# The two copies that empty a group's turned logits are handed out ahead of the next unit's two mask copies

## The chip, the cores and the metric

One core of a Trainium2 chip runs the whole program. The metric is the device time of one execution in microseconds (us); lower is better. Before the change the median of three runs is 447.19 us.

## What is computed

Three layers follow one another on 3072 tokens (4 batches of 768) of width 384 (8 heads of 48):

```python
# 1: a linear recurrence over time, per batch and head, state D x D
y[t]  = r[t] @ (state + (u * k[t]) outer v[t])
state = w * state + k[t] outer v[t]
# 2: soft mixture, 8 experts of 4 slots = 32 slots
logits     = x @ phi                                   # 3072 x 32
slot_input = softmax(logits, over tokens).T @ x        # 32 x 384
slot_out   = relu(slot_input @ w1[e]) @ w2[e]
x          = softmax(logits, over slots) @ slot_out
# 3: an MLP
h = x @ w_in;  out = (h * sigmoid(1.702 * h)) @ w_out  # 384 -> 2048 -> 384
```

All is float32.

## The kernel before

**Layer 1 and the logits of layer 2** run in one loop over 24 units. A unit is 128 tokens of one batch, with all 8 heads; units of two batches alternate. The recurrence is computed in chunks: inside a unit by masked products (TensorE makes `pa`, a mask cuts it to the triangle, the result is `am`), across units by a state (`u_ps`, `sc`, `sbd`). The loop is software-pipelined: step `n` (L652, from -2 to 25) handles several units at different stages, as `st_a(n + 1)`, `st_v(n)`, `st_n(n - 1)`, `k_turn(n + 2)`. The order in which the code stands is the order on each engine's queue: nothing reorders it (a manual schedule), and an engine that waits at one instruction holds back all behind it.

The steps that matter here, in the order of one pass of the loop:

- `r_decay(n + 2)` (L493): VectorE scales `rt` of a later unit.
- `st_a(n + 1)` (L505 to L523): TensorE makes the masked products `pa` in two banks (L512); VectorE copies one bank into `am` under the mask (L516, a predicated copy), ScalarE copies the other bank (L519), and GpSimd cuts that one to the triangle (L520). `am` of unit `n + 1` is read by `st_v(n + 1)` (L612), one step of the loop later.
- `st_q(n + 1)` (L529, L532): TensorE sums for the bonus term into `k_ps`, ScalarE copies them to `qT`.
- `bonus`, `st_n` (L547, L551), `k_turn` (L499, L502, L503), `st_y`, `st_u`, `st_v`, `st_s`, `st_x`.

Every four units make a **group** `g` of the mixture's logits. Its work is spread over two steps of the loop. In the first one (`n = 4g + 5`) TensorE makes the logits, `maxima` takes their running maximum and the exponentials `et`, and `rows(g, (0,))` turns `et` and the plain logits `ls` on TensorE into one bank, `ltp` (L204, L205). In the second (`n = 4g + 6`) `rows(g, (1,))` empties this bank by two copies: VectorE takes the exponentials to `en` (L209), ScalarE the logits to `lnat` (L210). Then `sums(g, ..., n=(0,))` makes the weighted sums `pp` on TensorE from `en` (L221). `lp`, `ltp`, `pp` are one after the other in the same bank (tag `l`, one buffer), so `pp` waits for both copies. In the instruction order before, ScalarE's copy `lnat` carries a wait for VectorE, whose copy `en` reads the same bank; and `bonus(n)` on GpSimd writes the `xn` slot that `pp` reads, so it waits for `pp`. Groups 0 to 4 go this way, at n = 6, 10, 14, 18 and 22; group 5 is handled behind the loop by `slot_inputs`.

In the same loop VectorE and ScalarE decode `w_in` (L87 to L107, three steps a pass) and SyncE hands out the loads of the weights.

**After the loop** come a branch on a flag (L711, its body is skipped with these inputs), the experts, whose weights and `w_out` are loaded meanwhile, and the **MLP**, which is two thirds of the time and a nearly unbroken row of matmuls (L1124).

Of the kernel before, what the change touches and what calls it, by code (L numbers as in the profile page):

```python
# [21 lines left out]
def attn_moe_mlp_kernel(  # L22
# [275 lines left out]
    with ExitStack() as actx:  # L298
# [60 lines left out]
        with tc.manual_schedule():  # L359
# [119 lines left out]
            def ok(i):  # L479
                return 0 <= i < NU  # L480
# [3 lines left out]
            def k_decay(i, eng=nc.gpsimd):  # L484
                if ok(i):
                    eng.tensor_tensor(
                        out=kp[i % NKP][:, :, 0:D], in0=kv[i % NKV][:, 0], in1=tab, op=ALU.mult
                    )

            def r_decay(i):  # L490
                if ok(i):
                    x = rt[i % NRT]
                    tt(out=x, in0=x, in1=tr, op=ALU.mult)  # L493

            def k_turn(i):

                if ok(i):
                    for q in range(NP):
                        nc.tensor.transpose(  # L499
                            k_ps[:, q, :], kp[i % NKP][:, 2 * q:2 * q + 2, :].rearrange("p h d -> p (h d)"), ident  # L500
                        )
                    nc.scalar.copy(out=kT, in_=k_ps)  # L502
                    tt(out=rk, in0=rt[i % NRT], in1=k_ps, op=ALU.mult)  # L503

            def st_a(i):  # L505

                if ok(i):
                    t = [ps.tile([P, NP, P], F32, tag="a", name="pa", bufs=2) for _ in range(2)]
                    for q in range(NP):
                        for m in range(2):  # L510
                            p = slice(HP * m, HP * m + D)
                            nc.tensor.matmul(  # L512
                                t[m][:, q, :], kT[p, q, :], rt[i % NRT][p, q, :], start=True, stop=True
                            )
                    x = am[i % NA]
                    nc.vector.copy_predicated(  # L516
                        out=x[:, 0], mask=mask.unsqueeze(1).to_broadcast([P, NP, P]), data=t[0]
                    )
                    nc.scalar.copy(out=x[:, 1], in_=t[1])  # L519
                    nc.gpsimd.affine_select(  # L520
                        out=x[:, 1], in_=x[:, 1], pattern=[[0, NP], [1, P]], compare_op=ALU.is_gt, fill=0.0,
                        base=0, channel_multiplier=-1,
                    )  # L523

            def st_q(i):

                if ok(i):
                    for q in range(NP):
                        nc.tensor.matmul(  # L529
                            k_ps[NS * q:NS * q + NS, 0, :], ubd[:, q, :], rk[:, q, :], start=True, stop=True  # L530
                        )
                    nc.scalar.copy(out=qT, in_=k_ps[:, 0, :])  # L532

            def bonus(i):
                if ok(i):
                    nc.gpsimd.tensor_tensor(
                        out=xn[:, i % NXN, 0:DM].rearrange("p (q m d) -> p q m d", m=2, d=D),
                        in0=kv[i % NKV][:, 1].rearrange("p (q m) d -> p q m d", m=2),
                        in1=xq[(i - 1) % NXT][:, DM:].rearrange("p (q m) -> p q m", m=2)
                        .unsqueeze(3).to_broadcast([P, NP, 2, D]), op=ALU.mult,  # L540
                    )

            def st_n(i):

                if ok(i):
                    for q in range(NP):
                        nc.tensor.transpose(  # L547
                            n_ps[:, 2 * q:2 * q + 2, :].rearrange("p h d -> p (h d)"), yT[:, q, :], ident
                        )
                    x = xn[:, i % NXN, 0:DM].rearrange("p (h d) -> p h d", d=D)  # L550
                    tt(out=x, in0=n_ps[:, :, 0:D], in1=x, op=ALU.add)  # L551
# [17 lines left out]
            def st_u(i):  # L569
                if ok(i) and units[i][1] < NC - 1:  # L570
                    for q in range(NP):
                        for m in range(2):
                            h = 2 * q + m
                            nc.tensor.matmul(
                                u_ps[HP * m:HP * m + HP, q, :], kp[i % NKP][:, h, :], kv[i % NKV][:, 1, h, :],
                                start=True, stop=True,
                            )

            def st_s(i):

                if not ok(i) or units[i][1] == NC - 1:
                    return
                b, c = units[i]
                s = sc[b % 2]
                wb = w128.unsqueeze(2).to_broadcast([P, NP, D])
                if c == 0:
                    tt(out=s, in0=u_ps, in1=wb, op=ALU.mult)
                else:
                    tt(out=s, in0=u_ps, in1=s, op=ALU.add)
                    tt(out=s, in0=s, in1=wb, op=ALU.mult)  # L590
                for m in range(2):
                    p = slice(HP * m, HP * m + HP)
                    nc.scalar.copy(out=sbd[b % 2][p, :, m, 0:D], in_=s[p])

            def st_y(i):
                if not ok(i):
                    return
                b, c = units[i]
                if c > 0:
                    for q in range(NP):  # L600
                        nc.tensor.matmul(  # L601
                            y_ps[:, q, :], sbd[b % 2][:, q].rearrange("p m d -> p (m d)"), rt[i % NRT][:, q, :],
                            start=(q == 0), stop=False, skip_group_check=True,
                        )

            def st_v(i):
                if not ok(i):
                    return
                c = units[i][1]
                for q in range(NP):  # L610
                    for m in range(2):
                        nc.tensor.matmul(  # L612
                            y_ps[HP * m:HP * m + D, q, :], kv[i % NKV][:, 1, 2 * q + m, :], am[i % NA][:, m, q, :],
                            start=(c == 0 and q == 0), stop=(q == NP - 1), skip_group_check=True,
                        )
                nc.scalar.copy(out=yT, in_=y_ps)  # L616

            def g1(g):
                grp.products(
                    g,  # L620
                    [[(phn[:, kk, :], xq[(4 * g + m + 1) % NXT][:, kk * P:(kk + 1) * P]) for kk in range(KD)]
                     for m in range(4)],
                )

            def g3_x(g):
                return [xn[:, (4 * g + m) % NXN, :] for m in range(4)]
# [25 lines left out]
            for n in range(-2, NU + 2):  # L652
                g, m = divmod(n - 5, 4)
                first, second = (0 <= g < NG and m == x for x in range(2))
                second = second and g < NG - 1
                r_decay(n + 2)
                st_a(n + 1)
                if second:
                    grp.rows(g, (1,))
                st_q(n + 1)  # L660
                if first:
                    g1(g)
                if second:
                    grp.sums(g, g3_x(g), n=(0,))
                bonus(n)
                st_n(n - 1)
                k_turn(n + 2)
                if first:
                    grp.maxima(g)
                if second:  # L670
                    grp.sums(g, None, n=(1,))
                st_y(n)
                st_u(n)
                st_v(n)
                st_s(n)
                st_x(n)
                if first and g < NG - 1:
                    grp.rows(g, (0,))
                k_decay(n + 3, nc.gpsimd if n > -1 else nc.vector)
                if n == 1:  # L680
                    flag()
                    flag_out()
                    selector()
                if n == 4:
                    n_ok = nc.values_load(flg, min_val=0, max_val=P * NP)
                if n >= 0:
                    ld_r(n + NRT)
                    ld_kv(n + NKV)
                wload(n)
                if n == NU - 1:  # L690
                    while eq:
                        load_w(*eq[0], wts, eq[0][0])
                        eq.pop(0)
                    for a in (2, 3):
                        load_w(NSL, a, wts, NSL)
# [514 lines left out]
```

## Time and profile before

| | |
|---|---|
| runs | 447.01, 447.19, 450.7 us |
| profiled execution | 451.58 us, of which the span of its instructions is 450.1 us |
| mean granted TensorE clock | 0.968 of full speed |
| busy, share of the span | TensorE 93%, VectorE 59%, ScalarE 42%, GpSimd 14% |
| the loop over the units | up to about 172 us of the span |
| branch, experts, loading of `w_out` | about 172 to 224 us |
| MLP | about 224 us to the end |

In the rows further down, times are microseconds from the span's start. A row of the timeline gives the start, the duration, the engine, the line, the operation with its output and inputs, and in square brackets how long the engine had been idle before it and whom it waited for. Starts of consecutive instructions on VectorE and ScalarE may lie a few hundredths of a microsecond before the end of the one ahead. PE is TensorE, PEld its weight loads, DVE VectorE, ACT ScalarE, POOL GpSimd, SPq the queue of SyncE that issues DMAs.

### The profile page before, as it was taken

Reading aid. Unit: us, or ns where it says so; the run is one execution under the profiler, and the core shown is the slowest. Engines: PE = TensorE matmul, PEld = TensorE weight load, DVE = VectorE, ACT = ScalarE, POOL = GpSimd, SP = SyncE. Lnnn points to the kernel's source line nnn. Section 1 sums busy time; section 2 is a strip of 40 time slices with the busy share of each in tenths; the row PEclk is TensorE's granted clock in tenths of the full one; section 3 lists DMA queues with packets and bytes.
Section 4 is the critical chain, followed back from the end, with each engine's and each line's share of the span. In section 5 each row is a group of like instructions: output and inputs, shape, how many; then the busy total and the mean of one; then the engine's idle time right before and its main releaser. Section 6 shows DMA issues by size and latency. Waiting matters only on the chain.

```text
span 450.1 us, 9164 instructions
## 1 busy us (share of the span) xinstructions
PE 417.3 (93%) x3704; PEld 363.0 (81%) x3704; DVE 265.3 (59%) x497; ACT 189.3 (42%) x444; POOL 61.0 (14%) x89
## 2 busy tenths in 40 slices
PE   7899899898989976996799999999999999999996
PEld 5687687676767853442499999999999999999996
DVE  6467788777879754304669995444454444544442
ACT  3345655455555631423458776222242222322321
POOL 4244334342433220000000000000000000000000
PEclk9589999999999998898999999999999999999999
DMA  7345788777867364799233200200011000110003
GB/s 253 114 146 178 254 267 274 235 257 259 270 223 233 109 229 163 252 381 379 93 109 108 69 1 6 100 0 1 0 46 61 1 0 1 66 40 0 1 0 106
DMA packets 36000, 59.50 MB, mean 132 GB/s; under 512 B 3056, under 2 KB 21616, under 8 KB 35952
## 3 DMA queue, kind: packets, MB, share of 16 engines
q1 hardware_dynamic: 35952, 58.85, 39.2%
q8 instruction: 32, 0.52, 0.5%
q14 instruction: 16, 0.13, 0.1%
HBM read 53.53 MB, written 4.72 MB: 129 GB/s over the span
## 4 chain that ended last, share of the span: by engine, by line
PE 54%; DMA 2%; DVE 2%; ACT 1%; SPq 1%; issue 1%; DVEq 0%; ACTq 0%
PE o L1124 45%; PE hpa L1062 3%; DMA raw_a<-in_moe_w_out_dram 2%; PE hp L819 2%; PE hpb L1062 2%; PE sop L843 1%; SPq L906 1%; PE htp L831 0%; ACT ggb L1065 0%; ACT G L1046 0%; PE ctp L883 0%; DVE lnat L865 0%; DVE w_lo L936 0%; DVE wtmp L103 0%; ACT c L869 0%
## 5 line engine op out<-in xcount | busy, mean ns | idle before, releaser
L1124 PE MATMUL o<-w_hi,ghb 128*128 128x384 f32 x384 | 116.7, 337 | 0.0
L1124 PE MATMUL o<-w_lo,ghb 128*128 128x384 f32 x384 | 116.4, 337 | 0.0
L1124 PE MATMUL o<-w_hi,glb 128*128 128x384 f32 x384 | 115.6, 334 | 0.0
L1065 ACT ACTIVATE ggb<-hpa 128x512 f32<-128x512 f32 x64 | 38.3, 598 | 118.7 <-PE hpa L1062 118.5
L1075 DVE CAST ghb<-ggb 128x768 fp32r<-128x768 f32 x48 | 26.9, 560 | 83.9 <-ACT ggb L1065 83.9
L1124 PEld LDWEIGHTS o<-w_hi,ghb 128*128 128x128 f32 x384 | 71.0, 190 | 2.5
L1124 PEld LDWEIGHTS o<-w_lo,ghb 128*128 128x128 f32 x384 | 71.7, 190 | 0.0
L1124 PEld LDWEIGHTS o<-w_hi,glb 128*128 128x128 f32 x384 | 71.1, 188 | 0.0
L1076 DVE TENSOR_TENSOR glb<-ggb,ghb 128x768 fp32r<-128x768 f32 x64 | 61.3, 957 | 13.1 <-ACT ghb L1073 11.5
L512 PE MATMUL pa<-rt,kT 48*128 48x128 f32 x384 | 29.7, 297 | 1.2 <-ACT kT L502 1.2
L512 PEld LDWEIGHTS pa<-rt,kT 48*128 48x128 f32 x384 | 24.9, 199 | 5.4 <-issue 3.4
L616 ACT COPY yT<-y_ps 128x512 f32<-128x512 f32 x24 | 14.0, 584 | 34.4 <-PE y_ps L612 34.4
L503 DVE TENSOR_TENSOR rk<-rt,k_ps 128x512 f32<-128x512 f32 x24 | 16.5, 688 | 18.5 <-ACT kT L502 18.5
L1062 PE MATMUL hpa<-c4T,G 96*128 96x512 f32 x64 | 25.4, 396 | 2.1 <-DVE G L1090 1.0
L520 POOL TENSOR_SCALAR_AFFINE_SELECT am<-am 128x512 f32<-128x512 f32 x24 | 15.6, 652 | 74.8 <-ACT am L519 71.0
L502 ACT COPY kT<-k_ps 128x512 f32<-128x512 f32 x24 | 14.1, 586 | 26.7 <-PE k_ps L499 26.7
L1065 ACT ACTIVATE ggb<-hpb 128x256 f32<-128x256 f32 x64 | 24.2, 378 | 0.0
L612 PE MATMUL y_ps<-am,stage 128*48 128x128 f32 x320 | 22.0, 281 | 0.0
L551 DVE TENSOR_TENSOR xn<-n_ps,xn 128x384 f32<-128x384 f32 x24 | 13.3, 554 | 13.5 <-PE n_ps L547 13.0
L601 PE MATMUL y_ps<-rt,sbd 128*128 128x128 f32 x160 | 21.1, 275 | 0.0
L499 PE MATMUL k_ps<-ident,kp 128*128 128x128 f32 x96 | 15.9, 291 | 5.6 <-ACT qT L532 4.0
L516 DVE COPY_PREDICATED am<-mask,pa 128x512 f32<-128x512 int32 x24 | 17.4, 726 | 3.8 <-PE pa L512 3.6
(181 smaller groups left out, 604.7 us busy)
## 6 DMA issues: line engine op xcount, KB each, us to landing
w<-in_moe_w_dram SPq DMA_DIRECT2D x32, 768.0 KB, 7.2
stage<-in_kv_dram SPq DMA_DIRECT2D x20, 384.0 KB, 3.9
rt<-in_rT_dram SPq DMA_DIRECT2D x24, 256.0 KB, 3.9
raw<-in_moe_w_in_dram SPq DMA_DIRECT2D x16, 384.0 KB, 4.1
out_dram<-obuf SPq DMA_DIRECT2D x24, 192.0 KB, 2.0
raw_a<-in_moe_w_out_dram SPq DMA_DIRECT2D x10, 384.0 KB, 3.5
raw_b<-in_moe_w_out_dram SPq DMA_DIRECT2D x6, 384.0 KB, 6.0
kv<-in_kv_dram SPq DMA_DIRECT2D x4, 384.0 KB, 3.5
```

Source lines behind the costliest of these rows:

```text
L499: nc.tensor.transpose(k_ps[:, q, :], kp[i % NKP][:, 2 * q:2 * q + 2, :].rearrange("p h d -> p (h d)"), ident)
L503: tt(out=rk, in0=rt[i % NRT], in1=k_ps, op=ALU.mult)
L512: nc.tensor.matmul(t[m][:, q, :], kT[p, q, :], rt[i % NRT][p, q, :], start=True, stop=True)
L516: nc.vector.copy_predicated(out=x[:, 0], mask=mask.unsqueeze(1).to_broadcast([P, NP, P]), data=t[0])
L520: nc.gpsimd.affine_select(out=x[:, 1], in_=x[:, 1], pattern=[[0, NP], [1, P]], compare_op=ALU.is_gt, fill=0.0, base=0, channel_multiplier=-1,)
L601: nc.tensor.matmul(y_ps[:, q, :], sbd[b % 2][:, q].rearrange("p m d -> p (m d)"), rt[i % NRT][:, q, :], start=(q == 0), stop=False, skip_g ...
L612: nc.tensor.matmul(y_ps[HP * m:HP * m + D, q, :], kv[i % NKV][:, 1, 2 * q + m, :], am[i % NA][:, m, q, :], start=(c == 0 and q == 0), stop ...
L1062: nc.tensor.matmul(hp, G4[:, f * P:(f + 1) * P], c4T[:, c * TB + t0:c * TB + t0 + n], start=True, stop=True)
L1065: nc.scalar.activation(out=ggb[:, i % NB_S, t0:t0 + n], in_=hp, func=AF.Gelu_apprx_sigmoid)
L1075: nc.vector.tensor_copy(out=gh, in_=gg)
L1076: nc.vector.tensor_tensor(out=gl, in0=gg, in1=gh.bitcast(F32), op=ALU.subtract)
L1124: nc.tensor.matmul(o, x, y, start=f == 0 and i == 0, stop=f == KF - 1 and i == 2)
```

## The change

`grp.rows(g, (1,))` stands one line higher, ahead of `st_a(n + 1)`. Its two copies come ahead of the two mask copies on VectorE and ScalarE in the five steps n = 6, 10, 14, 18 and 22. Nothing is added or removed, and the order on TensorE, GpSimd and SyncE is the same.

```diff
                 r_decay(n + 2)
-                st_a(n + 1)
                 if second:
                     grp.rows(g, (1,))
+                st_a(n + 1)
                 st_q(n + 1)
                 if first:
                     g1(g)
                 if second:
                     grp.sums(g, g3_x(g), n=(0,))
```

On VectorE, in the step n = 10 (group 1), the row of `rt` is `r_decay`, that of `am` the predicated copy, that of `en` the copy out of the turned logits, and that of `xn` the add of `st_n`:

```order
 L94 TENSOR_SCALAR win<-raw_94 128x3x128
 L493 TENSOR_TENSOR rt_105<-rt_105,tr 128x512
-L516 COPY_PREDICATED am_114<-mask,pa 128x512
-L209 COPY en<-ltp 128x128
+L209 COPY en<-ltp 128x128
+L516 COPY_PREDICATED am_114<-mask,pa 128x512
 L551 TENSOR_TENSOR xn<-n_ps,xn 128x384
 L503 TENSOR_TENSOR rk<-rt_105,k_ps 128x512
```

The copy `en` changed places with the predicated copy, and all around them stands where it stood; the other four groups show the same piece.

On ScalarE, in the same step before the change (`sq` belongs to the decoding of `w_in`, `am` is the second mask copy, `qT` that of `st_q`, `kT` that of `k_turn`):

```order
100 L87 ACTIVATE sq<-raw_94 128x384 [waits DMAHW1_49,DVE_49,Activation_49]
101 L519 COPY am_114<-pa 128x512 [waits PE_49,Pool_49]
102 L210 COPY lnat<-ltp 128x128 [waits DVE_49]
103 L532 COPY qT<-k_ps 128x128 [waits PE_49,Activation_49]
104 L502 COPY kT<-k_ps 128x512 [waits PE_49,Activation_49]
```

and after it:

```order
100 L87 ACTIVATE sq<-raw_94 128x384 [waits DMAHW1_49,DVE_49,Activation_49]
101 L210 COPY lnat<-ltp 128x128 [waits DVE_49]
102 L519 COPY am_114<-pa 128x512 [waits PE_49,Pool_49]
103 L532 COPY qT<-k_ps 128x128 [waits PE_49,Activation_49]
104 L502 COPY kT<-k_ps 128x512 [waits PE_49,Activation_49]
```

The copy `lnat` stands ahead of the second mask copy and keeps its wait for VectorE.

## Rows read from the trace of the kernel before

**Rows 1.** Busy time by stretch: each engine (instructions), granted clock, DMA share, GB/s.
```profile
core 0: us, PE busy (x) PEld busy (x) DVE busy (x) ACT busy (x) POOL busy (x), PEclk, DMA share, GB/s
...
75.00:100.00 25.00, 22.65 (x309) 17.95 (x307) 19.02 (x37) 13.50 (x35) 10.15 (x14) 1.00 0.77 251
...
172.00:185.00 13.00, 9.41 (x100) 5.43 (x92) 4.70 (x12) 3.38 (x7) 0.00 (x0) 0.74 0.32 104
```

**Rows 2.** Who waited for whom: us in total, times, longest us.
```profile
PE pp L221 <- ACT lnat L210: 7.7, 5, 2.0
...
ACT lnat L210 <- DVE en L209: 2.5, 4, 0.8
```

**Rows 3.** Timeline of the step n = 10, around group 1's turned logits.
```profile
80.09 0.68 DVE L493 TENSOR_TENSOR rt<-rt,tr 128x512 f32<-128x512 f32 x1
80.43 0.57 ACT L519 COPY am<-pa 128x512 f32<-128x512 f32 x1
80.69 0.72 DVE L516 COPY_PREDICATED am<-mask,pa 128x512 f32<-128x512 int32 x1
81.08 0.63 POOL L520 TENSOR_SCALAR_AFFINE_SELECT am<-am 128x512 f32<-128x512 f32 x1 [3.11 <-ACT am L519]
81.30 0.28 DVE L209 COPY en<-ltp 128x128 f32<-128x128 f32 x1
81.61 0.27 ACT L210 COPY lnat<-ltp 128x128 f32<-128x128 f32 x1 [0.60 <-DVE en L209]
81.77 0.27 ACT L532 COPY qT<-k_ps 128x128 f32<-128x128 f32 x1
...
81.93 0.85 PE L221 MATMUL pp<-xn,en 128*32 128x385 f32 x8 [2.00 <-ACT lnat L210]
...
82.85 0.83 POOL L536 TENSOR_TENSOR xn<-stage,xq 128x384 f32<-128x384 f32 x1 [1.14 <-PE pp L221]
...
83.20 0.60 PE L499 MATMUL k_ps<-ident,kp 128*128 128x128 f32 x4
83.47 0.56 DVE L551 TENSOR_TENSOR xn<-n_ps,xn 128x384 f32<-128x384 f32 x1 [1.90 <-PE n_ps L547]
```

**Rows 4.** Timeline at the same place of groups 0, 2 and 3.
```profile
53.65 0.72 DVE L516 COPY_PREDICATED am<-mask,pa 128x512 f32<-128x512 int32 x1
...
54.26 0.27 DVE L209 COPY en<-ltp 128x128 f32<-128x128 f32 x1
...
104.42 0.72 DVE L516 COPY_PREDICATED am<-mask,pa 128x512 f32<-128x512 int32 x1
104.69 0.57 ACT L519 COPY am<-pa 128x512 f32<-128x512 f32 x1
105.03 0.28 DVE L209 COPY en<-ltp 128x128 f32<-128x128 f32 x1
...
131.46 0.71 DVE L516 COPY_PREDICATED am<-mask,pa 128x512 f32<-128x512 int32 x1
...
132.07 0.27 DVE L209 COPY en<-ltp 128x128 f32<-128x128 f32 x1
```

**Rows 5.** Timeline at the same place of group 4, with its turning.
```profile
156.00 0.27 PE L205 MATMUL ltp<-ident,ls 128*128 128x128 f32 x1
...
156.73 0.55 DVE L94 TENSOR_SCALAR win<-raw 128x384 int32<-128x384 int32 x1
...
157.81 0.57 ACT L519 COPY am<-pa 128x512 f32<-128x512 f32 x1
...
158.34 0.27 ACT L210 COPY lnat<-ltp 128x128 f32<-128x128 f32 x1
```

**Rows 6.** Timeline of SyncE's queue behind the loop.
```profile
166.41 15.36 SPq L137 DMA_DIRECT2D w<-in_moe_w_dram  x2
181.88 1.83 SPq L145 DMA_DIRECT2D w<-in_moe_w_dram  x2
```

**Rows 7.** Timeline of the first expert's matmuls behind the branch.
```profile
177.82 5.11 PE L819 MATMUL hp<-w,sinT 128*32 128x256 f32 x48 [3.59 <-PEq L711]
```

**Rows 8.** Chain that ended last: a later expert's matmuls, and a load of `w_out`.
```profile
189.85 1.29 PE hp L819 x24
...
202.53 10.62 DMA raw_a<-in_moe_w_out_dram
```

## The prediction

> **What bounds the kernel now.** I read the busy time by stretch first. In the loop over the units, 75 to 100 us for instance, TensorE is busy 22.65 of 25 us, VectorE 19.02, ScalarE 13.50 and GpSimd 10.15, at the full granted clock of 1.00 [rows 1]. No engine is full, so the loop is a ring of short waits, and each wait that lies on the ring is worth its whole length. The list of waits comes next. TensorE waits 7.7 us in all, in five places, for `lnat`, before it may begin `pp`; ScalarE in turn waits for `en` on VectorE [rows 2]. These five places are the five steps that the change touches. The timeline shows one of them from inside [rows 3]: VectorE ends `r_decay`, begins the predicated copy at 80.69, begins `en` at 81.30, `lnat` begins at 81.61, 0.03 us behind the end of `en`, and `pp` at 81.93, after TensorE has stood still for 2.00 us. So `en` waits for nothing but its turn on VectorE, `lnat` for `en`, `pp` for `lnat`.
>
> After `pp` everything hangs on TensorE: the add `xn` on VectorE has waited 1.90 us for it, GpSimd's `bonus` 1.14 us, and the turning `k_ps` comes later still, at 83.20 [rows 3]. No engine runs ahead on a path that goes past `pp`. That makes `pp` a narrow gate: what it gains, all that follows gains.
>
> **The change part by part.** Ten instructions change places: five copies `en` with five predicated copies on VectorE, five copies `lnat` with five mask copies on ScalarE. None is added, removed or made longer, and no DMA moves, since SyncE's order is the same.
>
> *VectorE.* In groups 0 to 3 `en` takes the slot in which the predicated copy begins now. It needs the turned logits, which TensorE makes at the end of the step before. The tightest of the five is group 4, where they end at 156.27 and VectorE is not free before 157.28 [rows 5], so no new wait arises. The start moves from 54.26 to 53.65, from 105.03 to 104.42, from 132.07 to 131.46 [rows 4] and from 81.30 to 80.69 [rows 3]: four times 0.61 us.
>
> *ScalarE.* `lnat` now comes ahead of the mask copy, so ScalarE must be free for it. In group 1 it is free at 80.43, when the mask copy begins now, and `en` would end at 80.97, so `lnat` begins at 81.00 in place of 81.61 [rows 3]: the full 0.61. In group 2 ScalarE is free at 104.69 and `en` ends at 104.70 [rows 4]: full as well. In group 4 there is no `r_decay`; `en` could begin at 157.28 and end by 157.55, but ScalarE is only free at 157.81, where the mask copy stands now, and `lnat` moves from 158.34 to there [rows 5]: 0.53.
>
> *The sum.* `pp` begins about 0.31 us after `lnat` in either order, so TensorE gains 4 x 0.61 + 0.53 = 2.97 us of the 7.7 that it waits. What is left, 4.7 us, is the wait for `r_decay` and the decoding ahead of it, which the change doesn't touch.
>
> *What is put later.* The predicated copy begins one `en` later, at 80.97, and ends at 81.69. VectorE's next work is the add `xn`, which would start at 83.47 - 0.61 = 82.86: the cover is 1.17 us, so I take nothing. The mask copy on ScalarE begins behind `lnat`, at 81.27 at the latest, and ends at 81.84; `qT` behind it ends by 82.11. The turning into `k_ps`, which needs `qT` to be out, would begin at 83.20 - 0.61 = 82.59: a cover of 0.48, nothing again. GpSimd cuts the triangle from 81.92 to 82.55 at the latest in place of 81.08 to 81.71, and `bonus` behind it begins then, 0.30 us earlier than now rather than 0.61. `bonus` and the triangle are first read one step of the loop later, several us off. Were any of these covers gone, the delays to pay would be at most 0.28 on VectorE or 0.84 on ScalarE and GpSimd a group. All times of this paragraph come from [rows 3].
>
> *From the loop to the end.* The next question is whether the loop's gain survives the loading stage. SyncE stands at one issue from 166.41 for 15.36 us, until the first expert's matmuls have been evacuated, and hands out the next loads at 181.88 [rows 6]; DMA works at only 0.32 of its capacity from 172 to 185 [rows 1]. The loads whose end is waited for later, among them the 10.62 us of `w_out` on the chain that ended last [rows 8], start behind that issue. They hang on the end of the loop, and move forward with it. So the loads hide none of the gain. As bounds I keep both ends: nothing of it, if the loads had a fixed date, and all of it. I take all of it, because the queue itself shows that it waits for compute and not for a transfer.
>
> The sum is made on the profiled execution: 451.58 us, a span of 450.1 and 1.48 around it, becomes 448.6. That execution is 4.4 us above the median of the three runs, and one of these, at 450.7, is near it. The five waits lie in a part of the loop that runs at the full clock in the profile, so I take the same 2.97 us from the median: 447.19 - 2.97 = **444.2 us**, 0.7% faster.
>
> *The clock, weighed.* Behind the loop the 48 matmuls of the first experts take 5.11 us after TensorE has been idle for 3.59 [rows 7], 0.106 us each, while 24 such matmuls later take 1.29 [rows 8], 0.054 each: the first go at 1.2 GHz, the later ones at 2.4. In the stretch from 172 to 185 the granted clock is 0.74 on average [rows 1]. At 2.4 GHz the 48 would have taken 2.58, so this low stretch costs 2.5 us. The Trainium skill, "TensorE: Matmul & The Clock Gate", section "Part 1: The HAM clock gate (the "warmup" mystery)", says that TensorE's clock is gated by how busy the engine has been recently, and that the point of the change varies from run to run. The trace agrees with the first half by the rows just named; one profile can't show the second. By the row in the loop, 1.00, there is no clock to win back from shorter waits, and the sum stays 444.2; by the page the start of the low stretch against the shifted work could fall otherwise, and the sum would be 441.7 to 446.7.
>
> **The rivals.**
>
> *The clock takes it back, or adds to it.* The branch and the experts come 3 us earlier, and the low stretch behind the branch falls otherwise upon the matmuls. Its price is known from above: one more such stretch costs 2.5 us, 446.7 in all; one less, 441.7. For it speaks that the three runs of one and the same program lie 3.7 us apart. Against it: the idle time ahead of the low stretch is as long as before, whenever it comes. I give 0.12 to a loss and 0.07 to a gain.
>
> *The gain is hidden.* Something else sets the end of the loop or of the loads, and the 2.97 us become waiting elsewhere: 447.2. For it: DMA moves 251 GB/s in the loop [rows 1], so a late load is thinkable. Against it: VectorE and GpSimd wait for `pp` and its successors and not for a load [rows 3], and SyncE's queue waits for compute [rows 6]. 0.08.
>
> *The masks come too late: slower.* ScalarE's mask copy now stands behind a copy that waits for VectorE, and GpSimd's triangle behind that: up to 0.84 us later in each of five steps. If TensorE's next use of `am`, or of what GpSimd does next, had no cover, TensorE would lose 0.84 where it gains up to 0.61, and if it lost the gain too, 5 x 0.84 = 4.2 us would come on top of today's time: 451.4. The point from which it decides is a reader of `am` that comes less than 0.84 us after the triangle's end now, 81.71. Against it: TensorE's own order puts `pp`, the turnings and more between, up to 83.20 and beyond, before it comes to the next step [rows 3]. 0.03.
>
> **How the numbers follow.** The forecast, the full 2.97 us at an unchanged clock, has 0.70; with a loss to the clock 0.12, a gain from it 0.07, hidden 0.08, masks too late 0.03. The likeliest gives 444.2. The range goes from 443.2, where a part of a low stretch falls away, up to 447.2, the hidden case, which takes in the clock's loss at 446.7 too; outside lie the larger gain and the masks, 0.10 together. A measurement here tells about 1% from no change, which is 4.5 us: faster than 442.7 only with the clock's gain, 0.07; slower than 451.7 only if the masks cost a little more than their full price, 0.02; within 1% the rest, 0.91.
>
> **What would show it.** In the changed profile the wait of TensorE for `lnat` ahead of `pp` should fall from 7.7 to about 4.7 us in five places, to 1.39 in group 1. `lnat` should begin 0.03 us behind `en`, and `en` right behind `r_decay`. The span from one group's `pp` to the next should shrink by 0.6 us, and the first expert's matmuls should begin 3.0 us earlier, at about 174.9, as should the loads at 181.88. `xn`, L551, should still wait for TensorE, by about 1.2 us. I would be wrong if `pp` moved as said and the branch did not (a second ring beside this one), if the branch moved and the MLP did not (loads or clock), or if `qT`, L532, became what `k_ps` waits for.

## The result and the profile after

On the chip that timed the change, its median is 449.0 us over 15 runs, that of the kernel before 451.44 us over 15 runs. The ratio is 0.9889, with a 95% interval of 0.9845 to 0.9934: the change is faster by 1.1%, and the forecast of 0.7% (444.2 of 447.19, a ratio of 0.9933) lies at the interval's upper end. Applied to the 447.19 us of the prediction, the ratio gives 442.2 us, which is 1.0 us below the lower end of the stated range, 443.2; the interval, 440.3 to 444.2, reaches into the range. This ratio counts only the runs within 1.5% of the fastest of their kernel, 8 of the change's 15, all but one of them at a mean clock above 0.98; the means of all runs, 448.5 and 451.2 us, have a ratio of 0.9939.

Single runs of one and the same kernel lie far apart on this chip, from 443.1 to 453.7 us for the change and from 446.7 to 457.1 for the kernel before. That will matter below. The profiled execution of the change took 449.0 us with a span of 447.5.

The list of waits of the changed kernel (who waited for whom, total us, times, longest) answers to [rows 2]:

```profile
PE pp L221 <- ACT lnat L210: 4.7, 5, 1.4
...
ACT lnat L210 <- DVE en L209: 2.1, 4, 0.8
...
POOL xn L536 <- PE pp L221: 0.4, 1, 0.4
```

The 7.7 us have become the forecast 4.7. GpSimd's `bonus` hardly waits for `pp` any more: it now comes behind the triangle, as the bound of the prediction had it.

The timeline of the step n = 10 in the changed kernel answers to [rows 3] (start, us, engine, line, operation, idle time and whom it waited for):

```profile
78.96 0.69 DVE L493 TENSOR_TENSOR rt<-rt,tr 128x512 f32<-128x512 f32 x1
79.56 0.29 DVE L209 COPY en<-ltp 128x128 f32<-128x128 f32 x1
79.76 0.73 DVE L516 COPY_PREDICATED am<-mask,pa 128x512 f32<-128x512 int32 x1
79.88 0.27 ACT L210 COPY lnat<-ltp 128x128 f32<-128x128 f32 x1 [0.49 <-DVE en L209]
80.05 0.59 ACT L519 COPY am<-pa 128x512 f32<-128x512 f32 x1
...
80.20 0.85 PE L221 MATMUL pp<-xn,en 128*32 128x385 f32 x8 [1.40 <-ACT lnat L210]
80.52 0.28 ACT L532 COPY qT<-k_ps 128x128 f32<-128x128 f32 x1
80.71 0.63 POOL L520 TENSOR_SCALAR_AFFINE_SELECT am<-am 128x512 f32<-128x512 f32 x1 [3.87 <-ACT am L519]
...
81.31 0.83 POOL L536 TENSOR_TENSOR xn<-stage,xq 128x384 f32<-128x384 f32 x1
...
81.48 0.60 PE L499 MATMUL k_ps<-ident,kp 128*128 128x128 f32 x4
81.75 0.56 DVE L551 TENSOR_TENSOR xn<-n_ps,xn 128x384 f32<-128x384 f32 x1 [1.26 <-PE n_ps L547]
```

From the start of `r_decay` to the start of `pp` it was 80.09 to 81.93, 1.84 us; now it is 78.96 to 80.20, 1.24. The predicated copy ends at 80.49 and VectorE still waits 1.26 us for TensorE; `qT` is out at 80.80, well before `k_ps` at 81.48. So the later masks lie under cover, as worked out.

The same engine's rows for `pp` in the groups 0 to 5, changed kernel, with the first expert's matmuls:

```profile
53.84 0.85 PE L221 MATMUL pp<-xn,en 128*32 128x385 f32 x8 [0.91 <-ACT lnat L210]
...
80.20 0.85 PE L221 MATMUL pp<-xn,en 128*32 128x385 f32 x8 [1.40 <-ACT lnat L210]
...
103.30 1.51 PE L221 MATMUL pp<-xn,en 128*32 128x385 f32 x8 [0.64 <-ACT lnat L210]
...
131.29 0.85 PE L221 MATMUL pp<-xn,en 128*32 128x385 f32 x8 [1.40 <-ACT lnat L210]
...
156.65 0.85 PE L221 MATMUL pp<-xn,en 128*32 128x385 f32 x8 [0.39 <-ACT lnat L210]
...
169.75 0.85 PE L221 MATMUL pp<-xn,en 128*32 128x385 f32 x8
...
175.85 5.34 PE L819 MATMUL hp<-w,sinT 128*32 128x256 f32 x48 [3.62 <-PEq L711]
```

In the kernel before, the six `pp` began at 54.88, 81.93, 105.66, 132.70, 158.65 and 171.75. The distances between them went from 27.05, 23.73, 27.04, 25.95 and 13.10 us to 26.36, 23.10, 27.99, 25.36 and 13.10. Three of the four that should shrink did, by 0.69, 0.63 and 0.59. The third grew by 0.95, and its first row says why: the eight matmuls of `pp` at 103.30 take 1.51 us where all others take 0.85. Ahead of them TensorE had already waited once in this step, for `ls`:

```profile
100.78 0.33 PE L204 MATMUL ltp<-ident,et 128*128 128x128 f32 x1 [0.62 <-ACT ls L192]
```

The busy time by stretch around it, changed kernel (columns as in [rows 1]):

```profile
102.00:103.00 1.00, 0.66 (x14) 0.27 (x10) 1.00 (x4) 0.98 (x4) 0.00 (x0) 1.00 0.60 182
103.00:104.00 1.00, 0.70 (x8) 0.20 (x8) 0.58 (x1) 0.90 (x4) 0.19 (x1) 0.64 0.87 292
104.00:105.00 1.00, 1.00 (x9) 0.26 (x2) 0.00 (x0) 0.00 (x0) 0.56 (x2) 0.50 0.63 211
105.00:106.00 1.00, 1.00 (x6) 1.00 (x6) 0.03 (x1) 0.00 (x0) 0.71 (x1) 0.50 0.88 301
106.00:107.00 1.00, 1.00 (x8) 1.00 (x7) 0.53 (x1) 0.20 (x1) 0.00 (x0) 0.65 0.65 252
```

The granted clock fell to 0.50, the 1.2 GHz level, in the middle of the loop, behind a stretch in which TensorE had waited for `ls` and for `lnat`. The profile before had no such stretch there, though its waits at the same place were as long or longer:

```profile
102.53 0.33 PE L204 MATMUL ltp<-ident,et 128*128 128x128 f32 x1 [0.62 <-ACT ls L192]
...
105.66 0.85 PE L221 MATMUL pp<-xn,en 128*32 128x385 f32 x8 [1.24 <-ACT lnat L210]
```

The second profiled execution of the change (the run "The change again" below) has the low stretch again, at the same `pp`:

```profile
105.39 1.51 PE L221 MATMUL pp<-xn,en 128*32 128x385 f32 x8 [0.64 <-ACT lnat L210]
```

Behind the loop, SyncE's queue in the changed kernel hands out the next loads at 179.90, where it was 181.88 [rows 6]:

```profile
179.90 2.33 SPq L145 DMA_DIRECT2D w<-in_moe_w_dram  x2
```

### The profile page after: what moved, and what is told of

It is laid out like the page before. It is cut to its first block, busy times and chain, and to the rows that moved or that the text cites. A ratio compares the mean times of both kernels' runs of the same rounds, so it can differ in the third digit from the quotient of the medians.

```text
span 447.5 us, 9159 instructions
## 1 busy us (share of the span) xinstructions
PE 419.2 (94%) x3704; PEld 364.2 (81%) x3704; DVE 264.9 (59%) x497; ACT 188.7 (42%) x444; POOL 60.9 (14%) x89
## 4 chain that ended last, share of the span: by engine, by line
PE 53%; DVE 2%; DMA 2%; ACT 1%; issue 0%; SPq 0%; DVEq 0%
PE o L1124 43%; PE hpa L1062 3%; PE hp L819 2%; DMA raw_a<-in_moe_w_out_dram 2%; PE hpb L1062 2%; PE sop L843 1%; DVE glb L1076 1%; PE htp L831 0%; ACT raw_b L87 0%; PE s L1006 0%; DVE raw_a L107 0%; PE ga L1034 0%; ACT ggb L1065 0%; PE idle L995 0%; ACT G L1046 0%
## 5 line engine op out<-in xcount | busy, mean ns | idle before, releaser
L601 PEld LDWEIGHTS y_ps<-rt,sbd 128*128 128x128 f32 x160 | 19.6, 193 | 0.0
```

Of the source, the lines that this page charges most:

```text
L601: nc.tensor.matmul(y_ps[:, q, :], sbd[b % 2][:, q].rearrange("p m d -> p (m d)"), rt[i % NRT][:, q, :], start=(q == 0), stop=False, skip_g ...
```

## The experiments

Two readings are used. The first is the profile: TensorE's wait ahead of `pp`, and the distance from the first `pp` to the sixth, which leaves out the start and everything behind the loop (116.87 us in the kernel before).

The second takes the clock out of the times. Each run comes with its mean granted clock. In every kernel with many runs time falls with the clock: straight lines through the runs of the kernel before, on three occasions, and of the change have slopes of -2.9 to -3.9 us for 0.01 of clock. One common slope through all 157 runs, with a level for each kernel, comes to -3.3 us for 0.01, and the runs scatter by 1.0 us around it. The level of a kernel against that of the kernel before, with its 95% interval, is what "at the same clock" means below. The level uses every run, and is the better measure of small differences. It credits back all of a kernel's lost clock, also what the kernel itself may have cost.

| kernel | wait ahead of `pp`, us | first to sixth `pp`, us | ratio, 95% interval | mean clock (runs) | at the same clock, us |
|---|---|---|---|---|---|
| before | 7.7 | 116.87 | 1 | 0.9717 (57) | 0 |
| the change (both sets) | 4.7 | 115.91, low clock within | 0.9889 (0.9845 to 0.9934), 0.9888 (0.9818 to 0.9959) | 0.9754 (22) | -2.55 ± 0.49 |
| VectorE's half | 5.6 | 115.23 | 0.9907 (0.9843 to 0.9972) | 0.9692 (12) | -1.75 ± 0.62 |
| ScalarE's half | 6.3 | 115.64 | 1.0002 (0.9961 to 1.0043) | 0.9682 (12) | -0.86 ± 0.62 |
| late on the gate | 15.3 | 133.54, low clock within | 1.0314 (1.0234 to 1.0394) | 0.9443 (6) | +8.43 ± 0.97 |
| ahead of `r_decay` | 3.0 | 113.15 | 0.9799 (0.9727 to 0.9872) | 0.9783 (6) | -4.99 ± 0.84 |
| in the step before | 0.5 | 111.51 | 0.9781 (0.9699 to 0.9862) | 0.9782 (6) | -7.88 ± 0.84 |
| late behind the gate | 4.7 | 116.05, low clock within | 0.9927 (0.9868 to 0.9986) | 0.9735 (12) | -2.55 ± 0.62 |
| late but busy | 3.8 + filling | 122.95 | 1.0201 (1.0121 to 1.0282) | 0.9772 (6) | +7.54 ± 0.84 |
| before, kept busy | 2.7 + filling | 116.79 | 0.9961 (0.9921 to 1.0001) | 0.9787 (12) | +0.60 ± 0.63 |
| the change, kept busy | 2.4 + filling | 114.36 | 0.9860 (0.9795 to 0.9925) | 0.9857 (6) | -2.69 ± 0.87 |

**The change again**, beside the kernel before on another chip.

> The change itself once more, beside the kernel before on one chip, with the granted clock of each run. Theory A (the gate): compared at the same granted clock it is 2.97 us faster, TensorE's wait ahead of pp is 4.7 us; the plain ratio is 0.9935, moved by what the clock happens to be. Theory B (the clock made the gain): at the same clock the two are alike, and the plain ratio follows the clock alone.

The wait is 4.7 us again, the ratio 0.9888. Over both sets it is 2.55 us faster at the same clock, where theory A said 2.97 and theory B nothing: the gate made a gain of its own, and the interval, 2.06 to 3.04, holds the 2.97. The runs of this chip alone say the same, 2.5 ± 0.9 us.

**VectorE's half.** `rows` is split so that `en` (part 1) and `lnat` (part 2) can be placed apart.

```diff
                 r_decay(n + 2)
+                if second:
+                    grp.rows(g, (1,))
                 st_a(n + 1)
                 if second:
-                    grp.rows(g, (1,))
+                    grp.rows(g, (2,))
                 st_q(n + 1)
```

> Only VectorE's copy en goes ahead of its mask copy; ScalarE's copy lnat stays behind its own. Theory A (the start of pp is a gate, and VectorE's queue is what keeps it shut): lnat finds en already done and is only held by ScalarE's mask copy, so pp gains 0.61 us in groups 0, 1 and 3, about 0.18 in group 2 and 0.06 in group 4, where ScalarE is the later one: 2.1 us in all, TensorE's wait for lnat falls from 7.7 to 5.6 us, ratio to before 0.995. Theory B (what the change gained is the clock's chance, the waits are hidden later): the wait falls the same way, but the experts' first matmul comes no earlier than before, ratio 1.00. Theory C (the later mask copies cost something): this form keeps ScalarE's mask copy and GpSimd's triangle early, so it would come out as fast as the whole change or faster, 0.993 or less.

The list of waits of this kernel:

```profile
PE pp L223 <- ACT lnat L213: 5.6, 5, 1.4
```

Exactly the forecast, and the distance between the `pp` shrinks by 1.64 us where the groups 1 to 4 promised 1.46. The experts' first matmul follows:

```profile
177.54 5.14 PE L823 MATMUL hp<-w,sinT 128*32 128x256 f32 x48 [2.92 <-DVE lnat L859]
```

It begins 120.6 us behind the first `pp` (at 56.91), where it was 122.9 in the kernel before, and at the same clock the form is faster by 1.75 ± 0.62 us, so B falls. The plain ratio, 0.9907, holds the forecast within its interval, but would fit theory C too. Against C speaks the level: this form is 0.8 ± 0.7 us slower than the whole change.

**ScalarE's half.** Here `lnat` goes ahead and `en` stays.

```diff
                 r_decay(n + 2)
+                if second:
+                    grp.rows(g, (2,))
                 st_a(n + 1)
                 if second:
                     grp.rows(g, (1,))
                 st_q(n + 1)
```

> Only ScalarE's copy lnat goes ahead of its mask copy; VectorE's en stays behind the predicated copy. The order of the two reads of the bank turns round: en now waits for lnat, which is done long before. Theory A: pp waits for en alone, so what is saved is the step from the end of en to the end of lnat, about 0.31 us a group, 1.5 us in all, TensorE's wait goes to 6.2 us and names VectorE, ratio 0.9965. A theory by which the whole of the gain is VectorE's order says 0 here, 1.000. Theory B: 1.000 as well, with the wait shortened.

The list of waits of this kernel:

```profile
PE pp L223 <- DVE en L209: 6.3, 5, 1.7
```

The gate is now kept shut by VectorE, and the five waits are shorter by 1.4 us; between the first and the sixth `pp` it is 1.23 us, where four times 0.31 is 1.24. The plain ratio shows nothing, 1.0002, at the lowest clock but one of the table; at the same clock it is 0.86 us. So the plain time alone would have said that this half does nothing. Of the change's 3.0 us VectorE's order alone brings 2.1 by the waits, ScalarE's alone 1.4; the halves overlap, since both shorten the same row of two copies. That one copy must wait for the other at all fits the Trainium skill, "PSUM — Partial Sum Buffer", section "Terms": two engines on one bank and one quadrant of 32 partitions at the same time, two reads included, end in an error; both copies here read all 128 partitions of their bank. In the traces `lnat` starts 0.03 us behind the end of `en` in the one order; in the other, `lnat` ends 0.62 us before `en` begins in the step n = 10, so no wait is to be seen there, and no run here shows the error.

**Late on the gate**: the kernel before, with more work of VectorE ahead of `en`.

```diff
-                    nc.vector.copy_predicated(
-                        out=x[:, 0], mask=mask.unsqueeze(1).to_broadcast([P, NP, P]), data=t[0]
-                    )
+                    for _ in range(1 + more):          # more = 2 in the five steps, else 0
+                        nc.vector.copy_predicated(
+                            out=x[:, 0], mask=mask.unsqueeze(1).to_broadcast([P, NP, P]), data=t[0]
+                        )
```

> The kernel before, with the predicated copy made three times in the five steps n = 6, 10, 14, 18, 22, ahead of en: the opposite dose, the same data each time. Two more copies of 0.73 us, each waiting for the one ahead, put en later by about 1.5 us a group. Theory A: pp comes 1.5 us later each time, TensorE's wait grows from 7.7 to about 15 us, and the end moves by 7.5 us, ratio 1.017. Theory B: the wait grows but a good part of the 7.5 us is taken back behind the loop, ratio below 1.008.

The wait grew to 15.3 us, 7.6 more, as forecast. The time did not go by the forecast: it grew by 3.1%, 14 us, about twice the 7.5. From the first to the sixth `pp` it is 133.54 us, 16.7 more than before. The busy time by stretch around group 1's `pp` and TensorE's rows there:

```profile
86.00:88.00 2.00, 0.00 (x0) 0.00 (x0) 1.97 (x4) 0.92 (x2) 0.64 (x1) 0.84 0.69 204
88.00:90.00 2.00, 0.64 (x4) 0.20 (x8) 0.97 (x3) 0.43 (x2) 0.00 (x0) 0.50 0.95 346
90.00:92.00 2.00, 2.00 (x14) 1.20 (x7) 0.00 (x0) 0.00 (x0) 1.06 (x2) 0.50 0.17 62
92.00:94.00 2.00, 2.00 (x11) 2.00 (x10) 1.08 (x2) 0.59 (x1) 0.72 (x1) 0.50 0.01 2
```

```profile
89.36 1.51 PE L223 MATMUL pp<-xn,en 128*32 128x385 f32 x8 [3.51 <-ACT lnat L213]
90.80 1.12 PE L550 MATMUL n_ps<-ident,yT 128*128 128x128 f32 x4
91.71 1.06 PE L501 MATMUL k_ps<-ident,kp 128*128 128x128 f32 x4
```

Behind the wait of 3.51 us TensorE works at 1.2 GHz: `pp` takes 1.51 us for 0.85, the turnings 1.06 for 0.60. Such a stretch at 1.2 GHz follows each of the five waits, of 2.45 to 3.53 us. Over the loop, 50 to 172 us, the granted clock is 0.92, where it was 1.00. At the same clock the loss is 8.4 ± 1.0 us, close to the 7.6 of the waits.

**Late but busy**: the same, with idle transposes to keep TensorE at work while it waits.

```diff
                 st_q(n + 1)
+                if second:
+                    warmup(20, n_ps[:, 0:2, :].rearrange("p h d -> p (h d)"))
```

> e3 with 20 idle transposes into a free bank on TensorE, between the sums of st_q and pp in the five steps: TensorE is kept busy for about 2.2 us of the 2.5 to 3.5 that it waits there, and pp itself begins no later. Theory A with the clock as an amplifier: e3 cost 14 us where its waits add up to 7.5, because long idle times in the loop bring the granted clock down (0.92 from 50 to 172 us); with the idle time filled the loop's clock stays at 1.00, and the time goes to 7.5 us over the kernel before, 1.017. If the excess were the late start of what follows (masks, bonus), it would stay: 1.031.

The rows of TensorE around group 1's `pp`, and the loop's stretch from 50 to 172 us:

```profile
77.12 2.40 PE L377 MATMUL n_ps<-ident 128*128 128x128 f32 x20
80.73 0.85 PE L223 MATMUL pp<-xn,en 128*32 128x385 f32 x8 [1.20 <-ACT lnat L213]
```

```profile
50.00:172.00 122.00, 112.89 (x1482) 91.34 (x1480) 95.73 (x180) 61.22 (x161) 40.60 (x50) 1.00 0.69 220
```

The loop's clock is back at 1.00, the distance from first to sixth `pp` is 6.08 us longer than before for four groups, which is 1.52 each, where it was 16.7 longer without the filling, and the ratio falls from 1.031 to 1.020. At the same clock the loss is 7.5 us, the forecast. So the excess of the run before was the clock and not a second delay, and VectorE's masks, late here as well, cost nothing beyond the waits.

**Late behind the gate**: the change, with the same two added copies behind `en`.

```diff
                 r_decay(n + 2)
                 if second:
                     grp.rows(g, (1, 2))
-                st_a(n + 1)
+                st_a(n + 1, 2 if second else 0)
```

> The change, with the predicated copy made three times behind en: the same added work as in e3, but off the gate. Theory A: pp begins as in the change, TensorE's wait stays at 4.7 us; the last copy ends at about 83.1 by the times of group 1 where the add xn is due at 82.9, so xn comes up to 0.3 us late, which the wait of rk for kT behind it takes up. Ratio 0.9935 to 0.997, where e3, with the same copies ahead of en, had 1.031. A theory by which VectorE's load itself sets the loop expects the 7.5 us of the added copies less the 3 of the change, 1.010.

The timeline of the step n = 10 in this kernel:

```profile
75.82 0.28 DVE L209 COPY en<-ltp 128x128 f32<-128x128 f32 x1
76.02 2.27 DVE L519 COPY_PREDICATED am<-mask,pa 128x512 f32<-128x512 int32 x3
...
76.46 0.85 PE L223 MATMUL pp<-xn,en 128*32 128x385 f32 x8 [1.38 <-ACT lnat L213]
...
78.19 0.54 DVE L554 TENSOR_TENSOR xn<-n_ps,xn 128x384 f32<-128x384 f32 x1
...
79.05 0.69 DVE L505 TENSOR_TENSOR rk<-rt,k_ps 128x512 f32<-128x512 f32 x1 [0.32 <-ACT kT L504]
```

The three copies run to 78.29, VectorE's wait for `n_ps` is gone, and yet `rk` still waits 0.32 us for `kT`. The level is that of the change, -2.55 us, with 0.0 ± 0.7 us between the two; the plain ratio is 0.9927. The same 7.6 us of work on VectorE cost all of it ahead of the gate and nothing measurable behind it. That is the plainest sign of the cover that the prediction claimed on VectorE; ScalarE's and GpSimd's masks were not made longer in any run.

**Ahead of `r_decay`**: the two copies one step further forward.

```diff
+                if second:
+                    grp.rows(g, (1, 2))
                 r_decay(n + 2)
                 st_a(n + 1)
-                if second:
-                    grp.rows(g, (1, 2))
```

> Both copies go one step further forward, ahead of r_decay on VectorE. Theory A: en starts another 0.60 us earlier in groups 0 to 3, but ScalarE is not free before its mask copy's present start (53.46, 80.43, 104.69, 131.19 in the trace of before), so lnat gains another 0.50, 0.57, 0.04 and 0.58 us, and nothing in group 4, which has no r_decay: 1.7 us beyond the change, 4.7 in all, TensorE's wait falls to 3.0 us, ratio 0.9895. Theory B: as the change. Theory C: slower than the change, since rt of a later unit and both masks come later by 0.2 us more.

The wait is 3.0 us, as worked out, the level -5.0 us where 4.7 was forecast. The plain ratio, 0.9799, is again further down than the waits alone can take it; this kernel's clock was higher, 0.9783.

**In the step before**: the two copies right behind the turning.

```diff
                 st_a(n + 1)
-                if second:
-                    grp.rows(g, (1,))
                 st_q(n + 1)
 ...
                 if first and g < NG - 1:
                     grp.rows(g, (0,))
+                    grp.rows(g, (1, 2))
```

> Both copies are handed out at the end of the step before, right behind the turning (ahead of that step's decoding on VectorE and ScalarE). Theory A: en is out by 78.93 in group 1; lnat follows ScalarE's copies of xq, so by the trace of before it begins at 52.97, 79.95, 104.21, 130.71 and 157.32, and pp 0.31 us later, or when TensorE ends the sums of st_q at the earliest (53.37, 79.93, 104.42, 130.69, 157.73). TensorE's wait falls from 7.7 to about 0.8 us, the end comes 6.9 us earlier, ratio 0.9845. Theory D (VectorE is the next ring): with 1.7 us less a group the predicated copy ends when the add xn is due, and the end stops short of 6.9, nearer the 4.7 us of the form ahead of r_decay, 0.9895, with VectorE's wait for n_ps gone.

The list of waits of this kernel:

```profile
PE pp L223 <- ACT lnat L213: 0.5, 2, 0.2
...
DVE xn L553 <- PE n_ps L549: 3.8, 7, 1.1
```

The gate stands open: 0.5 us are left of 7.7. At the same clock the kernel is 7.9 ± 0.8 us faster than before, where 6.9 was forecast. VectorE's wait for `n_ps` has shrunk as theory D had it, from 13.0 us in 11 places to 3.8 in 7, but the gain doesn't stop at that of the form ahead of `r_decay`, so theory D falls. The ratio of 0.9781 makes it the fastest form of this study.

**Kept busy**: the kernel before with 8, and the change with 3 idle transposes ahead of `pp`, placed as above.

> The kernel before with 8 idle transposes on TensorE between the sums of st_q and pp in the five steps: about 0.9 us of its waits of 0.9 to 2.0 us are filled, and pp begins when it did. Theory A alone (the gate is all): nothing changes, ratio 1.000, mean granted clock as that of the kernel before on the same chip. Theory E (the waits also cost clock, which is where the change's measured ratio of 0.989 goes beyond 0.9935): the mean clock over the runs rises by some 0.004, and the time falls by 1.3 us, ratio 0.997, with the same time at the same clock.

> The change with 3 idle transposes at the same place, about 0.33 us of the 0.4 to 1.4 us that TensorE still waits there. Theory A: as the change, 2.7 to 3.0 us under the kernel before at the same granted clock. Theory E: a clock a little higher than that of the change, by less than in the kernel before, since there is less idle time to fill; the ratio goes from 0.989 to 0.987 at most. If neither form moves the mean clock, the clock's share in the measured ratio is chance.

In the kernel before the filling moves no `pp` (116.79 us from the first to the sixth) and costs nothing clear at the same clock, 0.6 ± 0.6. But the mean clock of its runs is 0.9787 for 0.9717, and the plain ratio 0.9961. With the change filled, the mean clock is 0.9857, the highest of all, and the distance of the `pp` is 2.51 us shorter than before: no low stretch blurs it here, and groups 1 to 4 were to bring 3 x 0.61 + 0.53 = 2.36. Both mean clocks go the way of theory E.

The traces don't. These are two stretches of the kernel before, and the same two of the kernel before, kept busy:

```profile
8.00:30.00 22.00, 19.56 (x196) 15.07 (x197) 12.79 (x26) 8.72 (x22) 6.18 (x9) 0.69 0.43 150
50.00:172.00 122.00, 108.47 (x1484) 85.87 (x1482) 93.91 (x185) 65.48 (x175) 42.26 (x53) 1.00 0.73 240
```

```profile
8.00:30.00 22.00, 19.14 (x269) 14.98 (x268) 15.32 (x31) 11.47 (x30) 7.96 (x10) 1.00 0.60 202
50.00:172.00 122.00, 111.32 (x1478) 88.22 (x1478) 92.63 (x182) 62.12 (x166) 40.72 (x51) 1.00 0.72 234
```

From 50 to 172 us, where the waits lie, the clock is 1.00 with and without the filling. What differs between these two executions is the clock from 8 to 30 us, 0.69 and 1.00. That stretch ends before the first filling, at 48.35, and its code is the same in both. "Late behind the gate", which has no filling, has 1.00 there too. So the higher clock of this profiled execution is not the filling's doing, and where the higher means of the other runs come from isn't shown. The two halves speak against theory E as well: their waits are shorter than those of the kernel before, and their mean clock is lower. Six or twelve runs with a spread of 0.01 in the clock don't settle how much clock the change itself won or lost.

## Why the prediction was right, and where it was not

- **The gate.** Right, and in numbers: 4.7 us of wait left, 1.40 in group 1 (1.39 said), the add `xn` still waiting 1.26 (1.2 said), three clean distances shorter by 0.69, 0.63 and 0.59 (0.61, 0.61 and 0.53 said). Six forms of the kernel with waits from 0.5 to 15.3 us have times, at the same clock, that move with the wait: -7.2 gives -7.9, -4.7 gives -5.0, -3.0 gives -2.55, -2.1 gives -1.75, -1.4 gives -0.86, +7.6 gives +8.4.
- **What is put later.** Right: the copies behind the gate cost nothing that the runs can tell, and VectorE's not even three times as long. For the masks on ScalarE and GpSimd the evidence is the changed trace, with its three clean distances and `qT` out before `k_ps`. With that the rival of the late masks is answered, and by the level of -2.55 us the hidden gain too.
- **From the loop to the end.** The queue of SyncE, that stood until 181.88 [rows 6], stands until 179.90 in the changed kernel. The loads moved with the loop. But I had named 174.9 us for the first expert's matmuls, and they began at 175.85, 1.97 us earlier than before where 2.97 were said. Of the 2.97 us, the low clock in the loop took 1.56 back in this execution (0.95 instead of -0.61 in one distance), and a start 0.43 us shorter gave some of it back. The MLP (half of the span, not two thirds as said in the part on the kernel before) moved with the branch: its long row of matmuls began at 223.65 in the kernel before and at 221.53 in the changed one, and the span ended 2.6 us earlier.

```profile
223.65 1.81 PE L1124 MATMUL o<-w_hi,ghb 128*128 128x384 f32 x5
```

```profile
221.53 1.05 PE L1124 MATMUL o<-w_hi,ghb 128*128 128x384 f32 x5
```

- **The clock: the step that failed.** The forecast took the gain "at an unchanged clock", since the loop's row showed 1.00. In both profiled executions of the change the clock in the loop did change: it fell to 1.2 GHz at group 2's `pp`, and one of the four distances grew by 0.95 us (by 1.02 in the second execution) where it was to shrink by 0.61. I had looked for the clock's risk behind the branch only. That waits in the loop can cost clock is shown by the late forms (0.92, and 1.00 when filled). Why it fell here, behind waits no longer than those of the kernel before, stays open.
- **The time beyond the forecast.** The measured ratio, 0.9889, is 2.0 us beyond the forecast, and no run shows that shorter waits won them. At the same clock the change gains 2.55 ± 0.49 us, and the means of all runs give 2.8 us; both agree with 2.97. The change's mean clock is higher by 0.0037, worth 1.2 us by the common slope, but the single runs of either kernel spread by about 0.01. So the sum held. The time beyond it is, as far as shown, luck with the clock; to a gain from there I had given 0.07.
- **The price of a low stretch.** The 2.5 us were read from a piece of the chain that begins inside its 24 matmuls. The timeline of the kernel before has all of them:

```profile
189.67 1.48 PE L819 MATMUL hp<-w,sinT 128*32 128x256 f32 x24
```

By this row the 48 would have taken 2.96 us, and the low stretch costs 2.15. That price, too, is for one stretch; the profiled executions have others that come and go, such as the one from 8 to 30 us.

## What to carry to other kernels

Look for the one instruction on which all engines come together, here the weighted sum of a group, and ask what stands ahead of its inputs on each queue that doesn't need to. Here work moved from ahead of such a gate to behind it was free where the next wait on its engine was longer; that wait could be read from the trace beforehand. And when runs of one kernel differ by more than the change is worth, compare all of them at the same granted clock, and read the gain from distances in the trace, but look first whether the clock fell within them. A higher mean clock is a gain of the change only if the trace shows it in the stretch that the change touches.

## What the runs showed of the hardware

One run's time follows its mean granted clock by 3.3 us for 0.01 on the common line; kernels with twelve runs or more have 2.6 to 3.9 by themselves. Where TensorE waits 3.5 us inside a loop that is otherwise dense, it comes back at 1.2 GHz: eight matmuls take 1.51 us for 0.85. The Trainium skill, "TensorE: Matmul & The Clock Gate", section "HAM oscillation — how this bites in real kernels", describes such waits between bursts as the cause of a falling clock, and the trace agrees. Not expected was that waits of 0.62 and 0.64 us came before such a fall too, in both profiled executions of the change, while the kernel before, with 0.62 and 1.24 us at the same place, shows none: the length of these waits alone doesn't tell when the clock falls. Nor was it expected that 20 transposes without any use, 2.40 us long, in each of the five waits of a kernel with late inputs brought its loop's clock from 0.92 to 1.00 and its ratio from 1.031 to 1.020. And one and the same code, from 8 to 30 us, ran at a granted clock of 0.61 to 1.00 in the twelve profiled executions.
